# Split attention with a max-gated feed-forward on one core: a new order of all queues, with other engines for some copies and other issuers for some stores

## The chip, the core and the metric

The kernel runs on one core of one Trainium2 chip. The metric is the device time of one execution in microseconds. The core has five engines that run side by side, each through its own queue in order: TensorE (PE, with its weight loads PEld), VectorE (DVE), ScalarE (ACT), GpSimd (POOL) and SyncE (SP), which only issues DMAs here. An instruction waits on semaphores for the results it needs; while it waits, everything behind it in the same queue waits too.

## The reference

Attention with two kinds of heads, and then a feed-forward whose gate is a maximum of two projections. All is float32.

```python
# q, k, v: (4 batches, 8 heads, 768 tokens, 64); heads 0, 2, 6 are "retrieval"
scores = q @ k.T / sqrt(64)
keep   = causal                                   # retrieval heads
keep   = causal & (first 4 keys | last 64 keys)   # the other five heads
x      = softmax(where(keep, scores, -1e9)) @ v   # -> (3072 tokens, 512)
h1, h2 = x @ w1, x @ w2                           # 512 -> 1024
out    = maximum(h1, h2) @ w_out                  # (3072, 512)
```

## The kernel before, in words

**The arithmetic.** Since max(h1, h2) = h2 + relu(h1 - h2), the kernel builds w12 = w1 - w2 (L1091, on DVE) and w2o = w2 @ w_out (transposes of w2 at L1108, products at L1135, both on PE) near its start. Then out = x @ w2o + relu(x @ w12) @ w_out: one up-projection in place of two. Everything on PE is bf16, accumulated in f32 in eight PSUM banks.

**The stages.** The 3072 tokens are worked in eight half-sequences of 384 tokens, in the order (batch, half) = (0,0), (1,0), (0,1), (1,1), (2,0), (2,1), (3,0), (3,1). In each half-sequence the heads go in four pairs; a table found at run time puts the three retrieval heads first. A half-sequence passes through these steps, and several of them are in flight at once:

- SP loads q, k and v (ld, L433 and L448); DVE, ACT or POOL cast them to bf16 (qb and vb, L368 on ACT and L370 on DVE or POOL).
- q and k are turned so that the head dimension lies on the partitions (qk). In batches 0 and 1 PE does it (L595) and DVE or ACT copy the result out of PSUM; in batches 2 and 3 a DMA transpose that SP issues does it (L618).
- For the windowed heads, small copies gather the keys and values of the sinks (kx on DVE, ACT or POOL; vx likewise, L368 and L370).
- PE computes scores (L846), ACT their exponentials (at, L861), DVE multiplies by the mask (L886), PE forms the weighted sums with a column of ones for the denominator (L911), DVE takes the reciprocal (rez, L928) and normalises into x (L938).
- x is turned into xt: by PE (L1055) and a copy for the first three half-sequences, by a DMA transpose from SP (L1074) for the other five.
- PE makes the up-projection: eight groups of four matmuls (L1158), each followed by a relu into g, on ACT (L1183) or DVE (L1185).
- For each of the three tiles of 128 tokens, PE sums four x-parts (x @ w2o) and eight g-parts (g @ w_out) into one bank (L1215); ACT or DVE copies it into one of four output buffers (ot, L368 or L370, the "take-out"), and SP, ACT or POOL issues the store (out_dram<-ot, L1243).

The four output buffers tie the end of a store to a later copy: take-out number n must wait until store number n - 4 has landed. Takes 13 to 19 are stored in two DMAs of half the width.

**The front.** Until the first loads have landed and been cast, PE works on dummy matmuls (L355). In the very first half-sequence the rows of v are spread over the partitions by matmuls with a shifted identity (L638).

**What sets the order.** The function `tile_three_full_heads` (L304) builds a list of 1089 operations with their dependencies. The order in which they are emitted is a string, `PLAN` (L158), with a second string, `LAST` (L213), for the operations behind a run-time branch near the end. `Order.run` (L140) walks the string. Each token is an operation's number, a letter for its engine (p PE, a ACT, v DVE, g POOL, s SP) and, where it claims PSUM, the banks; tokens with x or y are dummies. Each engine's queue is what this walk leaves it, so the string decides the order of all five queues, which of the allowed engines makes a copy, a cast or a relu, which issuer has a store, and which bank a result goes to.

```python
n = next(i for i, c in enumerate(token) if c.isalpha())
o, e, spots = self.ops[int(token[:n])], engines[token[n]], [int(c) for c in token[n + 1:]]
for key, m in o.claims:
    self.at[key] = spots[:m]
o.emit(e)
```

Numbers of operations that are spoken of later: 618 and 613 store the tiles 10 and 9 (batch 1, second half); 828 is the DMA transpose of q and k for the third pair of (3,0), 837 that of its fourth pair, and 705 that of the fourth pair of (2,1).

Of the kernel before, what the change touches and what calls it, by code (L numbers as in the profile page):

```python
# [163 lines left out]
101v 131p7 105v 10g 108p1 132v 109p 135p3 113p 15s 145p 136a 12g 114v 110v 111v 154p 116v 143p 112v 115v 146p
117p7 119p3 118a 144p 120v 148p 121v 150p 147a 155p 151a 125v 18s 211p2 209p1 213p3 133v 210a 215p7 214a 129v
17s 149a 224p0 216a 226p4 167a 195v 169g 222p1 197a 212a 156v 157g 220p3 223a 181v 19s 173p5 201p7 221v 219p2
202a 159v 23s 174v 198a 182g 158a 218p6 183g 225v 170a 184g 168a 196g 20s 227a 189p1 163p3 160a 187p7 190v 175p5
164a 203p0 191v 229p 176a 204v 21s 188a 179v 205v 165p4 177v 207v 252p13 193v 264p50 166v 253a 200g 426s 234p
265a 162g 161v 266a 199v 254a 172g 256p74 186a 240p15 206v 258a 260p03 171g 230p 262a 185v 178g 241a 267v 237p
24s 261a 208v 192v 242a 263v 247p43 244p10 257a 217p5 194v 243v 249a 259v 246a 268p7 228p 245a 22s 255v 248a  # L170
251v 180a 269p 250v 235a 279p3 270v 284p 278p0 272v 318g 309a 273p1 285v 286v 274p 319g 280p 299a 231p 271v 275v
293g 292a 276v 277v 238a 308g 322p4 424s 281v 282v 296p6 298g 232a 287v 312p7 283v 297a 323v 302p1 428s 290p2
288p3 303a 291v 359p50 289v 363p64 377s 366p21 365a 328p3 557s 360a 338p4 301v 295g 361a 304v 311g 332p5 294v
339a 300g 367a 340p0 306v 362v 556s 364a 330p4 326v 333a 334p2 368a 435v 429g 427s 313v 397p6 436g 335a 336p5
329a 305g 341v 439p1 320g 337a 321g 342p2 233s 331v 440a 452g 451v 425s 378p73 236g 381p05 314v 343v 372p41 379a
553s 398p 316v 382a 443v 399p 307g 354p2 374a 444v 325v 560s 373a 324v 447p7 327v 383a 355p 448v 380a 310a 555s
369p01 317a 441v 389p45 384v 315g 385p37 371a 356p 390a 431g 391a 445g 558s 349p1 430a 392v 386a 455p4 376v 239a
554s 433p5 453v 350p 370a 456v 387a 552s 400p 357a 375v 503p30 401v 388v 393p47 351p 394a 403v 508s 395a 404p2
674s 434a 405p 396v 410p4 406p 411p7 457v 504a 407v 416p 402v 559s 412p 344p5 413v 505a 409v 408v 414v 490p63
676s 417v 497p02 415v 491a 418v 345p 419v 352a 506v 585g 498a 420p4 507v 677s 422p6 562a 346p 421v 353g 492a  # L180
423v 499a 432g 512p71 347v 500p04 437g 494p36 502a 561g 465p2 493v 348s 454a 501a 568g 469p5 678s 496a 449v 575g
576v 467p4 675s 470a 567v 495a 565s 459p0 578g 466v 438a 577g 528p6 514a 468v 446g 529p 513a 458g 509p53 460v
673s 516p21 524p47 515v 518a 579s 584v 461p0 563v 587a 442v 511a 473p1 462v 517a 801s 530p 566v 463p3 569a 519v
588s 526a 531p 510a 471p0 532v 474v 525a 485p2 570s 464v 472a 533v 450a 520p75 624p14 682v 803s 522a 628p30 486p
521a 806s 629a 480p5 523v 625a 527v 683a 535p7 626a 541p3 686s 534v 542p1 536p 547p 537p 543p 548v 481p 550v
581g 538v 544v 549v 540v 482p 586g 545v 687g 539v 591v 487p 546v 694g 483a 580v 551s 582v 630a 592g 627v 475p6
572g 571v 636p41 648p73 802s 640p50 564v 638a 476p 573v 642a 488v 679s 641a 681s 639v 477p 590v 649a 688v 637a
589v 650a 652p1 478a 653p 651v 680s 739p02 643v 631p57 740a 644p43 603p6 632a 691s 741a 599p0 633a 597p5 583a
805s 645a 595p2 598v 807s 646a 605p7 574v 600v 804s 596a 647v 609p4 358a 634v 704g 662p5 635v 593p3 690g 757s
701g 607p0 594v 695g 657p2 606v 608a 484g 664p 601p3 698s 665v 703a 654v 656v 697a 663p7 604a 702g 602v 658p  # L190
668p 619p0 479a 659v 660v 705s 661v 610p 667v 655v 669v 833g 670v 620p 666v 816g 671v 692v 684g 672s 611p 742v
824g 743p63 612a 811g 699v 749p21 746p57 809s 750a 621p 696g 751a 808s 834g 748a 614p4 923s 622v 745a 744a 706v
615p 685v 815v 747a 925s 810v 761p21 758p73 765p06 760a 616p 814s 766a 714p5 836g 926s 716p3 715a 927s 767a
722p0 717v 837s 762a 777p5 617v 759a 720p6 723v 778p 819s 835v 721a 779p 700v 769p32 763a 839g 768v 773p47 770a
# [1486 lines left out]
```

## Time and profile before

| what | value |
|---|---|
| median of 3 runs | 176.64 us (176.63 to 176.72) |
| the profiled execution, whole | 176.57 us |
| its span, first to last instruction | 174.8 us |
| PE busy | 166.8 us |
| DVE, ACT, POOL busy | 123.8, 112.0, 49.0 us |
| moved by DMA | 37.31 MB, 213 GB/s on average |

A row of a group reads: line, engine, operation, output<-inputs, shapes and count, then the busy time, the mean of one in ns, and the idle time of the engine just before it, with what ended most of that. A row of a timeline reads: start and length in us, engine, line, operation, output<-inputs, count, and in brackets the idle time before it and what ended that. "SPq" is the time in which SP issues a DMA, not the transfer. The chain of waits is followed back from the last instruction; each row is a start, a length, and an engine with its line or a DMA. PE's rows name the line of the matmuls; DVE's, ACT's and POOL's copies all have the line of one helper (L370 and L368), so the names of the tiles tell them apart.

### The profile page before, as it was taken

The numbers are of one execution on the slowest core, as the hardware profiler recorded it, in microseconds if no ns is written. First come the engines' busy times: TensorE is split into PE (matmuls) and PEld (weight loads), VectorE is DVE, ScalarE is ACT, GpSimd is POOL, SyncE is SP. The second block draws the span as 40 slices with busy tenths as digits, with TensorE's granted clock in tenths as the row PEclk, the third lists the DMA queues.
The fourth block names the chain that finished last, engine by engine and source line by source line (L and its number), as shares of the span: only waits on it lengthen the run. The fifth ranks groups of instructions, "written<-read, shape, count | busy, mean of one in ns | idle before, by whom it ended". The sixth has DMA issues, their size and how long they took to land.

```text
span 174.8 us, 4672 instructions
## 1 busy us (share of the span) xinstructions
PE 166.8 (95%) x1686; PEld 96.0 (55%) x1686; DVE 123.8 (71%) x342; ACT 112.0 (64%) x248; POOL 49.0 (28%) x113
## 2 busy tenths in 40 slices
PE   7999999999799999999999999999799999999992
PEld 2456555654566575566466446663456456645541
DVE  5578969698997589985958954974678728934320
ACT  3399746889969998898394286905594699200501
POOL 5722130332563103700603260100670083000300
PEclk9999999999999999999999999999999999999999
DMA  4999999999999898699999999999989563040145
GB/s 130 334 371 387 388 381 334 213 291 327 231 246 286 186 270 196 188 163 207 197 217 255 268 158 223 156 246 199 237 220 190 90 164 126 0 90 4 59 130 180
DMA packets 83677, 37.31 MB, mean 213 GB/s; under 512 B 68290, under 2 KB 78530, under 8 KB 83650
## 3 DMA queue, kind: packets, MB, share of 16 engines
q1 hardware_dynamic: 81440, 32.19, 81.9%
q0 software_dynamic: 1056, 3.15, 5.5%
q10 hardware_dynamic: 1154, 1.64, 2.8%
q8 instruction: 14, 0.23, 0.6%
q14 instruction: 13, 0.11, 0.2%
HBM read 25.17 MB, written 6.29 MB: 180 GB/s over the span
## 4 chain that ended last, share of the span: by engine, by line
PE 64%; DMA 11%; DVE 10%; SPq 7%; ACT 3%; issue 3%; DVEq 0%; ACTq 0%
PE ps L1158 21%; PE ps L1215 21%; PE ps L846 6%; PE ps L911 6%; DVE x L938 4%; SPq L618 3%; DMA qk<-qb 3%; PE ps L1135 3%; DMA ld<-in_k_dram 3%; SPq L448 3%; DMA out_dram<-ot 2%; ACT at L861 2%; PE ps L595 2%; DMA ld<-in_v_dram 2%; DVE at L886 2%
## 5 line engine op out<-in xcount | busy, mean ns | idle before, releaser
L861 ACT ACTIVATE at<-ps 128x512 bf16<-128x512 f32 (+2 forms) x134 | 65.6, 568 | 18.0 <-PE ps L846 16.4
L1215 PE MATMUL ps<-wob,g 128*128 128x512 bf16 (+2 forms) x200 | 46.3, 371 | 0.0
L1158 PE MATMUL ps<-xt,w 128*128 128x384 bf16 x256 | 45.8, 326 | 0.3 <-DVE xt L370 0.2
L1158 PEld LDWEIGHTS <-w 128*128 128x128 bf16 x256 | 23.6, 98 | 16.8 <-issue 0.8
L886 DVE TENSOR_TENSOR at<-at,tab 128x1024 bf16<-128x1024 bf16 (+5 forms) x56 | 29.1, 544 | 5.1 <-ACT at L861 4.6
L1185 DVE TENSOR_SCALAR g<-ps 128x384 bf16<-128x384 f32 x35 | 18.5, 551 | 17.7 <-PE ps L1158 15.4
L1215 PEld LDWEIGHTS <-g 128*128 128x128 bf16 x200 | 17.7, 98 | 18.6 <-issue 0.6
L1183 ACT ACTIVATE g<-ps 128x384 bf16<-128x384 f32 x29 | 14.2, 497 | 19.8 <-PE ps L1158 19.8
L370 POOL CAST qb<-ld 128x384 bf16 (+1 forms) x32 | 14.6, 477 | 42.8 <-DMA ld<-in_q_dram 29.6
L1215 PE MATMUL ps<-w2o,xt 128*128 128x512 bf16 (+2 forms) x100 | 24.3, 371 | 0.0
L938 DVE TENSOR_TENSOR x<-ps,rez 128x192 f32 x64 | 22.8, 356 | 1.7
L911 PEld LDWEIGHTS <-at 128*128 128x128 bf16 x477 | 18.5, 97 | 5.7 <-DVE at L886 1.0
L846 PE MATMUL ps<-qk 64*128 64x128 bf16 (+1 forms) x322 | 18.7, 227 | 1.6 <-DVE ot L370 1.3
L911 PE MATMUL ps<-vb,at 128*128 128x65 bf16 x387 | 19.5, 193 | 0.4 <-DVE at L886 0.3
L846 PEld LDWEIGHTS <-qk 64*128 64x128 bf16 x322 | 11.6, 94 | 10.3 <-issue 7.9
L1243 POOL DMA_DIRECT2D out_dram<-ot x18 | 9.8, 550 | 20.2 <-ACT ot L368 20.2
L370 POOL CAST vb<-ld 128x192 bf16 x26 | 9.5, 390 | 20.2 <-DMA ld<-in_v_dram 20.1
L368 ACT COPY ot<-ps 128x512 f32<-128x512 f32 (+2 forms) x13 | 7.2, 555 | 12.1 <-PE ps L1215 11.7
L1215 PEld LDWEIGHTS <-xt 128*128 128x128 bf16 x100 | 9.1, 98 | 8.9
L370 POOL COPY vx<-vb 64x396 bf16<-64x396 bf16 (+4 forms) x14 | 7.1, 511 | 21.0 <-ACT vb L368 10.4
L370 DVE COPY ot<-ps 128x512 f32<-128x512 f32 x12 | 8.1, 686 | 6.8 <-DMA out_dram<-ot 4.4
L370 DVE COPY kx<-qk 128x192 bf16<-128x192 bf16 (+5 forms) x33 | 8.5, 265 | 5.5 <-DMA qk<-qb 5.1
(76 smaller groups left out, 160.4 us busy)
## 6 DMA issues: line engine op xcount, KB each, us to landing
ld<-in_v_dram SPq DMA_DIRECT2D x21, 256.0 KB, 5.0
ld<-in_moe_w_dram SPq DMA_DIRECT2D x4, 1024.0 KB, 11.2
ld<-in_k_dram SPq DMA_DIRECT2D x4, 768.0 KB, 8.6
ld<-in_q_dram SPq DMA_DIRECT2D x4, 768.0 KB, 7.1
ld<-in_k_dram SPq DMA_DIRECT2D x12, 256.0 KB, 4.4
ld<-in_q_dram SPq DMA_DIRECT2D x12, 256.0 KB, 5.0
ld<-in_moe_w_out_dram SPq DMA_DIRECT2D x4, 512.0 KB, 6.2
out_dram<-ot POOLq DMA_DIRECT2D x6, 256.0 KB, 3.5
```

What stands on the lines that cost most here:

```text
L368: nc.scalar.copy(out=out, in_=in_)
L370: eng[e].tensor_copy(out=out, in_=in_)
L846: nc.tensor.matmul(to.rearrange("p (i c) -> p i c", c=128), lhsT=lhsT, rhs=rhs, start=True, stop=True, skip_group_check=True,)
L861: nc.scalar.activation(out=at[:, bk, 0:w], in_=bank(("ps", b, hf, t), part=bk)[:, 0:w], func=ACT.Exp, scale=scale,)
L886: eng[e].tensor_tensor(out=at, in0=at, in1=tbl, op=ALU.mult)
L911: nc.tensor.matmul(po[:, hh, i - NT * hf, :], lhsT=ats[:, T["at", b, hf, t] % NAT, bk, e * 128:(e + 1) * 128], rhs=rhs, start=first, stop= ...
L938: nc.vector.tensor_tensor(out=xs[:, HALVES.index((b, hf)) % NX, :, bass.ds(heads[2 * p + hh], 1), :], in0=po[:, hh, :, 0:D].unsqueeze(2), ...
L1158: nc.tensor.matmul(bank(key)[:, 0:HALF], lhsT=w[:, kc, fc * 128:(fc + 1) * 128], rhs=xts[:, HALVES.index((b, hf)) % NXT, :, kc, :], start= ...
L1183: nc.scalar.activation(out=g, in_=ph, func=ACT.Relu)
L1185: nc.vector.tensor_scalar_max(out=g, in0=ph, scalar1=0.0)
L1215: nc.tensor.matmul(bank(key)[:, cols], lhsT=lhsT, rhs=(w2o if kind == "x" else wob)[:, c, cols], start=(e == 0), stop=(e == len(steps) - 1),)
L1243: queues[e].dma_start(out=out[r0:r0 + 128, lo:lo + n], in_=ots[:, number % NOUT, lo:lo + n])
```

## The change

Only the strings `PLAN` and `LAST` are replaced. The list of operations and their dependencies are the same, and so is every function.

```diff
 PLAN = """
-1s y0 0s y0 2s y0 y1*3 y2*3 3s y3*3 y4 29a 51v y4 57a 59v y4 49a 67v y5 27v 65g 54p0 62p1 y7 55v 25g y7 y2*2 y7
...
+0s y0 1s y0 2s y0 y1*2 3s y1 y2*3 y3*3 28a 64v y4*2 48v y4 26v y5 58v y5 50g y5 y6*3 y7*2 49a 29v 51g y7 27a
...
 LAST = """
-1074v 1068p 1075a 1077p 1069v 1078p 1070s 1081p5 1079a 1082p 1083p 1080s 1084a 1085a
+1069a 1074v 1077p 1070s 1078p 1075s 1081p7 1079a 1082p 1083p 1080s 1084a 1085a
```

By engine, DVE has 311 operations in place of 316, ACT 272 in place of 253, POOL 76 in place of 91, SP 94 in place of 93. PE has the same operations with 30 dummies in place of 27. Of the relus ACT has 36 in place of 29, of the take-outs 16 in place of 13, and DVE the rest. Of the stores SP has 7 in place of 6, ACT 9 in place of 7, POOL 9 in place of 12, not always the same ones. The first load is of q, not of k.

SP's queue in the part in which the first loads and transposes of the last two batches' second halves are issued, before the change. The transposes of qk are L618, that of x is L1074, the stores are L1243:

```order
L618 DMA_TRANSPOSE qk<-qb 128x6x128
L448 DMA ld<-in_k_dram 128x8x64 x2
L618 DMA_TRANSPOSE qk<-qb 128x6x128 x2
L1243 DMA out_dram<-ot 128x512
L448 DMA ld<-in_v_dram 128x8x64
L448 DMA ld<-in_q_dram 128x8x64
L618 DMA_TRANSPOSE qk<-qb 128x6x128
L1243 DMA out_dram<-ot 128x512
L448 DMA ld<-in_q_dram 128x8x64
L1074 DMA_TRANSPOSE xt<-x 128x12x128
```

The same part of SP's queue after the change:

```order
L1074 DMA_TRANSPOSE xt<-x 128x12x128
L448 DMA ld<-in_q_dram 128x8x64
L618 DMA_TRANSPOSE qk<-qb 128x6x128 x3
L448 DMA ld<-in_k_dram 128x8x64
L448 DMA ld<-in_q_dram 128x8x64 x2
L448 DMA ld<-in_k_dram 128x8x64
L618 DMA_TRANSPOSE qk<-qb 128x6x128
L448 DMA ld<-in_k_dram 128x8x64
L618 DMA_TRANSPOSE qk<-qb 128x6x128
L448 DMA ld<-in_v_dram 128x8x64
L1074 DMA_TRANSPOSE xt<-x 128x12x128
```

The two stores (613 and 618) are no longer in SP's queue. The transpose 705, which stood ahead of the first rows shown of before, is the second of the three in the third row shown of after, behind the xt, the q load and the transpose 837.

POOL's queue after the change, around the stores that it takes over; qb and vb are casts, vx is a copy of sink values:

```order
L370 COPY vx<-vb 64x198
L1243 DMA out_dram<-ot 128x512
L370 ISA
L370 COPY qb<-ld 128x6x64
L370 ISA
L370 COPY vb<-ld 128x3x64
L370 COPY vx<-vb 64x2x198
L370 ISA
L370 COPY vb<-ld 128x3x64
L1243 DMA out_dram<-ot 128x512
```

The first of the two is 618, the second 613. Each stands in POOL's queue among casts that wait for loads.

ACT's queue in the last stage, before the change, up to the run-time branch; g is a relu, ot a take-out:

```order
L1183 ACTIVATE g<-ps_163 128x384
L1183 ACTIVATE g<-ps_160 128x384
L368 COPY ot<-ps_158 128x512
L1183 ACTIVATE g<-ps_161 128x384
L1183 ACTIVATE g<-ps_163 128x384
L1243 DMA out_dram<-ot 128x256 x2
```

The same part after the change:

```order
L368 COPY ot<-ps_157 128x512
L1183 ACTIVATE g<-ps_158 128x384
L1243 DMA out_dram<-ot 128x256 x2
L368 COPY ot<-ps_156 128x512
L1183 ACTIVATE g<-ps_162 128x384
L1183 ACTIVATE g<-ps_160 128x384
L368 COPY ot<-ps_161 128x512
L1183 ACTIVATE g<-ps_157 128x384
L1243 DMA out_dram<-ot 128x256 x2
L1183 ACTIVATE g<-ps_159 128x384
L1183 ACTIVATE g<-ps_162 128x384
L1183 ACTIVATE g<-ps_156 128x384
```

Four of the last eight relus were ACT's; now seven are, with two take-outs and two stores in two parts standing between them, and DVE has one.

More of the change, by code (lines that the diff above doesn't have):

```diff
@@ L164 @@
[L164 to L193, printed above, removed]
@@ new lines @@
+79v 137p0 84v 94a 88v 97p5 140p 90a 96v 99p 91a 139p4 100v 107p2 102v 98p1 130a 92v 141p 142p 134v 131p3 101v
+109p 10v 103p 132a 135p5 153p 104v 15s 106v 136a 110v 108p3 111v 113p 145p 112v 12a 143p 114v 116v 144p 115v
+154p 105v 17s 150p 117p5 121v 119p2 146p 120a 148p 118v 155p 125v 211p3 156a 18s 209p1 129v 213p2 215p5 212v
+133v 222p6 216a 19s 210a 220p3 223a 224p5 167a 159v 214a 147v 226p1 157a 197v 169a 218p6 181v 195a 183v 221a
+225v 149a 20s 201p2 163p0 151v 187p3 219p5 182a 198g 170a 168g 188v 196a 21s 184g 227a 202v 173p7 158g 203p4
@@ new lines @@
+160a 175p3 189p1 204v 174a 229p 22s 190a 205v 164v 176a 264p27 207v 191v 165p4 265a 193v 260p13 23s 177v 266a
+172g 252p02 166v 199a 234p 171g 254a 162g 186a 267v 200a 185g 261a 256p74 255v 230p 161g 258a 194v 179v 428s
+257a 180v 208v 247p21 192v 262a 237p 259v 248a 263v 253a 278p4 249a 280p 244p73 250v 24s 240p20 281v 178a 206v
+217p1 241a 292v 282v 242a 251v 279p2 283v 284p 228p 245a 285v 243v 235a 424s 287v 246a 273p0 236g 293v 298a
+268p4 286v 269p 274p 238a 296p7 309g 270v 426s 275v 231p 272v 318a 319g 276v 297a 308g 271v 322p6 553s 299g 277v
@@ new lines @@
+429v 387a 437v 375v 394a 558s 378p73 376v 389p45 457v 380a 431v 350p 401v 388v 379a 395a 351p 402v 403v 390a
+557s 396v 404p6 391a 433p3 384v 410p7 352a 392v 405p 560s 412p 434a 344p1 413v 414v 441v 508s 411p2 415v 416p
+406p 417v 490p45 559s 407v 503p03 409v 491a 345p 353s 408v 504a 418v 492a 675s 419v 500p74 494p60 420p2 566g
+496a 422p5 561g 421v 346p 423a 442g 562v 239a 576g 465p0 347v 505a 565s 567g 463p2 495a 585v 466a 432v 459p5
+464v 502a 673s 506v 501a 512p31 509p60 568g 493v 676s 513a 497p24 461p7 510a 348s 454v 575v 511a 469p3 458g 449v
@@ new lines @@
+777p6 612v 837s 614p7 759a 693g 760a 703v 615p 751a 813v 750a 778p 705s 826a 779p 780p 761p45 781v 765p21 835v
+752p03 814s 616p 753a 763a 710p0 617a 927s 720p5 754a 711v 924s 618g 767a 712p7 764v 923s 825g 840v 766a 782v
+716p3 704g 783v 816a 926s 706v 768v 714p0 707a 721v 708p1 717a 819s 755v 836a 838v 718p2 697v 709a 713v 700g
+762a 769p65 715v 893p31 818g 770a 773p74 613g 722p0 771a 925s 774a 729p6 772v 828s 775a 756v 790p5 723a 791p7
+776v 784p4 894a 785p 786p 895a 792p 796p 787v 734p0 793v 719a 794v 930s 797v 789v 730p 799v 795v 731p 798v 788v
@@ new lines @@
+989a 906p2 941v 869p 866a 904v 946v 945a 905v 907p 870p 908v 915v 910v 1001p75 909v 992p03 991v 1002a 995p14
+921s 858p2 952v 996a 955v 1004v 956g 997a 859p 949v 871a 1006s 993a 860p 1003a 994a 1022p71 861v 998p46 1014p05
+1000a 1026p3 1005v 862g 1027p 999a 1028p 1023a 959p2 1015a 967p6 960v 1016a 1029p 1024a 971p4 968v 939a 1007p70
+972v 942g 1010p25 1018p61 1009a 1030v 957p4 1031v 1012a 1017v 1019a 961p0 1025v 1011a 963p5 958a 1013v 1020a
+1039p6 969p2 1008a 1021v 1033p4 970a 978p1 964a 962a 1040p7 1045p 1041p 1034p 1046v 1032v 1035p 965p2 1042v
```

47 lines of the change are left out of this document (26 added, 21 removed).

## The prediction

> **What bounds the kernel now.** I read the first page first: the span, the busy time of each engine and the chain that ended last.
>
> ```profile
> span 174.8 us, 4672 instructions
> PE 166.8 (95%) x1686; PEld 96.0 (55%) x1686; DVE 123.8 (71%) x342; ACT 112.0 (64%) x248; POOL 49.0 (28%) x113
> PE 64%; DMA 11%; DVE 10%; SPq 7%; ACT 3%; issue 3%; DVEq 0%; ACTq 0%
> ```
>
> PE is busy for 95% of the span, and no other engine passes 71%. The operations do not change, so PE's busy time cannot change by much either: an order can only win or lose in the 174.8 - 166.8 = 8.0 us in which PE does nothing, which include the start before the first matmul and the last store's way to memory. The list of waits says who holds PE, and what holds those in turn.
>
> ```profile
> PE ps L846 <- DVE ot L370: 1.3, 1, 1.3
> PE ps L1055 <- DVE x L938: 1.1, 3, 0.8
> ...
> DVE kx L370 <- DMA qk<-qb: 5.1, 3, 2.1
> ...
> DVE ot L370 <- DMA out_dram<-ot: 4.4, 2, 4.1
> ```
>
> PE's longest single wait is for a copy of an output tile (L370, ot) out of PSUM by DVE. The second is for normalised rows (L938, x) that it is to turn. DVE itself waits for two kinds of transfers: turned q and k (qk<-qb), and stores that free an output buffer (out_dram<-ot). The busy times by window show in which stages PE has room: columns are the window, its length, then the busy time of PE, PEld, DVE, ACT, POOL, the granted clock, the DMA share and GB/s.
>
> ```profile
> 27.10:49.70 22.60, 21.17 (x232) 13.02 (x232) 20.08 (x49) 17.83 (x44) 7.08 (x19) 1.00 1.06 278
> 105.70:125.60 19.90, 18.46 (x212) 10.76 (x213) 14.33 (x40) 10.43 (x26) 2.81 (x6) 1.00 1.24 211
> 158.60:171.60 13.00, 13.00 (x81) 7.26 (x79) 4.90 (x11) 2.71 (x6) 1.61 (x3) 1.00 0.23 77
> ```
>
> The first two leave PE idle for 1.43 and 1.44 us. The last stage has no hole at all: there a reorder can only lose. The clock is 1.00 throughout, so nothing is to be had from it.
>
> **Term a: the two stores that leave SP's queue (105 to 125 us).** These rows are SP's queue, DVE and PE around PE's longest wait, and the store's landing in the chain.
>
> ```profile
> 110.33 4.35 SPq L618 DMA_TRANSPOSE qk<-qb  x2
> ...
> 116.60 1.71 SPq L618 DMA_TRANSPOSE qk<-qb  x1
> 118.41 0.52 SPq L1243 DMA_DIRECT2D out_dram<-ot  x1
> ```
> ```profile
> 107.73 0.68 DVE L370 COPY ot<-ps 128x512 f32<-128x512 f32 x1
> ...
> 122.00 0.26 DVE L370 COPY kx<-qk 128x320 bf16<-128x320 bf16 x1 [2.11 <-DMA qk<-qb]
> ...
> 122.75 0.69 DVE L370 COPY ot<-ps 128x512 f32<-128x512 f32 x1 [0.24 <-DMA out_dram<-ot]
> ```
> ```profile
> 123.50 0.38 PE L846 MATMUL ps<-qk 64*128 64x128 bf16 x7 [1.25 <-DVE ot L370]
> ```
> ```profile
> 118.41 4.26 DMA out_dram<-ot
> ```
>
> The output tile was ready at 107.73 + 0.68 = 108.41, but its store stood in SP's queue behind transposes that take 1.7 to 2.2 us each to issue, and went at 118.41: 10.0 us in the queue, 4.26 us on the way. It landed at 122.67; the copy that needed its buffer began at 122.75, and PE's scores, which needed the bank emptied by that copy, had waited 1.25 us. In the new order this store (618) and the one before it (613) are POOL's, right behind the copies that fill them, and POOL is busy 28% of the span. The store then lands about 10 us earlier relative to its copy, long before the buffer is asked for again. But the same DVE queue also waited 2.11 us, until 122.00, for a transpose that SP issued at 116.60; without the store, the output copy could have begun at about 122.5, only 0.3 us sooner, had the transpose stayed where it is. The new order has SP issue this transpose (828) without stores ahead of it and with more PE work between it and its reader (5.6 us against 3.9, an estimate counted along PE's queue with the durations of this trace), which is as much as 1.7 us to set against that wait of 2.11. I take the stall as gone: -1.3. Bounds: 0, if the transpose's landing holds DVE as now; -1.4, all that the window leaves.
>
> Against this speaks the Trainium skill, "DMA: Bandwidth & Descriptors", section "Issuing engines are not separate DMA queues": transfers from any issuer share the same 16 engines, and spreading issuers saves only the issue time, usually small beside the transfer. By that rule term a is near 0, which is the first rival below. Here the trace disagrees on "small": 10.0 us in the queue against 4.26 on the way.
>
> **Term b: the turn after the second half-sequence (44 to 50 us).** The chain of waits there:
>
> ```profile
> 44.40 0.57 PE ps L911 x13
> ...
> 46.53 0.20 DVE rez L928
> ...
> 47.53 0.36 DVE x L938
> 47.89 0.52 DVE qk L370
> ...
> 49.74 4.06 PE ps L1158 x24
> ```
>
> After the last weighted sum at 44.97 DVE still has the normalisations of three tiles ahead of PE's turn, and copies of turned x behind it, until the next up-projection at 49.74. The new order leaves two tiles' normalisations (two instructions of 0.36 us fewer) behind the last weighted sum, turns the first two tiles first and gives ACT one of the copies of turned x. So -0.7. Bounds: -1.1 (all that PE waits for x at L1055) and 0, if another copy takes the place.
>
> **Term c: the front.** PE before 13 us:
>
> ```profile
> 1.15 5.52 PE L355 MATMUL ps<-warmer 128*128 128x512 bf16 x16 [1.15 <-POOL warmer L1606]
> 6.73 0.51 PE L595 MATMUL ps<-tab,qb 128*128 128x128 bf16 x6
> 7.08 1.89 PE L355 MATMUL ps<-warmer 128*128 128x512 bf16 x8
> ...
> 11.50 0.40 PE L846 MATMUL ps<-qk 64*128 64x128 bf16 x8
> 12.22 1.02 PE L638 MATMUL ps<-xt,g 128*128 128x512 bf16 x4 [0.33 <-DVE xt L370]
> ```
>
> Now 26 dummies stand ahead of the first turn, where 16 stood; by the rows the ten more end at about 1.15 + 5.52 + 10 x 0.23 = 9.0 us, where the first turn was at 6.73. The dummies fill time in which PE would wait for loads, so the three that are added (30 against 27) cost nothing by themselves. But the spreading of v (L638) waits for casts of v, at 12.22 as now, and ahead of it stands one group of scores where three stood: up to two groups of 0.40 us go behind it and are done later, of which I take about half: +0.4. Bounds +0.8 (both groups) and -0.3 (the 0.33 that PE waits there, if the casts come sooner).
>
> **Term d: the last stage.** ACT and DVE, PE's x-part of the down-projection, the two groups of ACT and the last store's issue:
>
> ```profile
> 162.65 0.87 ACT L1183 ACTIVATE g<-ps 128x384 bf16<-128x384 f32 x2 [12.80 <-PE ps L1158]
> ...
> 172.05 0.34 ACTq L1243 DMA_DIRECT2D out_dram<-ot  x1
> ```
> ```profile
> 163.95 1.49 DVE L1185 TENSOR_SCALAR g<-ps 128x384 bf16<-128x384 f32 x3 [2.36 <-PE ps L1158]
> ```
> ```profile
> 160.50 4.06 PE L1158 MATMUL ps<-xt,w 128*128 128x384 bf16 x24
> 164.40 1.89 PE L1215 MATMUL ps<-w2o,xt 128*128 128x512 bf16 x8
> ```
> ```profile
> L1183 ACT ACTIVATE g<-ps 128x384 bf16<-128x384 f32 x29 | 14.2, 497 | 19.8 <-PE ps L1158 19.8
> L368 ACT COPY ot<-ps 128x512 f32<-128x512 f32 x11 | 6.5, 588 | 5.9 <-PE ps L1215 5.7
> ```
>
> Today the last eight relus are four on each engine. In the new order ACT has seven, with two output copies and two stores in two parts between them: 7 x 0.50 + 2 x 0.59 + 4 x 0.34 = 6.0 us from the second up-projection's end. PE needs the last relu after six more ups and two x-parts, 4.06 + 1.89 = 5.95 us. ACT so ends level or a little late; with some 0.2 us from a matmul's end to a relu's start and as much back, +0.5. Bounds 0 (the g-parts take the late tile last) and +1.3 (the stores' waits for issue also fall between).
>
> **Term e: SP between 98 and 108 us.** SP, and DVE behind it:
>
> ```profile
> 98.08 3.69 SPq L618 DMA_TRANSPOSE qk<-qb  x2
> 101.86 1.47 SPq L1074 DMA_TRANSPOSE xt<-x  x1
> 103.38 1.53 SPq L448 DMA_DIRECT2D ld<-in_v_dram  x2
> ```
> ```profile
> 103.08 0.40 DVE L370 COPY kx<-qk 128x192 bf16<-128x192 bf16 x1 [2.04 <-DMA qk<-qb]
> ...
> 107.25 0.56 DVE L1185 TENSOR_SCALAR g<-ps 128x384 bf16<-128x384 f32 x1 [2.24 <-PE ps L1158]
> ```
>
> The second transpose at 98.08 (705, the last of the sixth half-sequence) is now put behind five transfers that followed it: the xt, two v loads, a q load and another transpose (837), at 1.47 + 1.53 + 0.8 + 1.9 = 5.7 us of issue. Its reader on DVE, the copy of kx, also stands later, but 4.4 us of PE work behind the issue where it was 5.0: 0.6 less cover. Behind that copy DVE holds relus of the running stage that PE waits for; today a wait of 2.04 costs PE nothing, for DVE then waits 2.24 us on PE. I take +0.4 of the missing 0.6; bounds 0 and +1.4.
>
> The rest goes together at 0: ACT takes 19 more operations and DVE 5 fewer, both below 75% busy; the remaining stores change issuers with PE work of over 3 us to cover them.
>
> **Sum.** -1.3 - 0.7 + 0.4 + 0.5 + 0.4 = -0.7. The profiled execution took 176.57 us, its span 174.8 and 1.77 around it; the median of the runs shown is 176.64, 0.07 above it. So the span becomes 174.1 and the time 175.9 us.
>
> **Rivals.**
> - The transpose's landing holds DVE at 120 us, not the store: term a is 0, the sum +0.6, the time 177.2. For it: the 2.11 us wait came first and the store's own 0.24 was on top. Against it: two stores leave the queue ahead of that transpose. Chance 0.17. By the rule of the Trainium skill in term a the time is this one too.
> - Slower, by one mechanism: the transpose 705 lands too late. If SP's slip is half as much again as the 5.7 us of issue (2.9 more), DVE holds the relus behind the copy for 2.9 - 0.6 = 2.3 us that PE sees; term e is +2.3 in place of +0.4, and the time is 175.9 + 1.9 = 177.8. It decides from a landing past about 110 us. For it: DVE's waits on these transposes are its largest on a transfer (5.1 us). Against it: two stores fewer in that queue. Chance 0.16.
> - All of the idle time in the two windows goes and nothing new comes: -1.4 - 1.1 = -2.5, 174.1 us. Against it: the last stage and the front offer new waits. Chance 0.12.
> - The new order does nothing that shows, since PE is 95% busy in both and the idle time only changes place: 176.6. Chance 0.10.
>
> **The numbers.** My forecast, 175.9, has the chance 0.45, with its own range of 175.0 to 177.0. A measurement of this kernel can tell 0.2%, 0.35 us, from no change: faster is below 176.29, slower above 176.99. Of the forecast's 0.45 some 0.35 is faster, 0.07 the same, 0.03 slower. With the third rival faster has 0.47; with the fourth and a part of the first (0.03) the same has 0.20; slower has 0.33. The range, 174.0 to 178.2, takes in the first two rivals with the 0.4 us that the other terms may add, and the third.
>
> **What would show it.** Term a: PE's wait on DVE's ot copy is gone from the list of waits, and the stores that POOL issues there land within 6 us of their copies. Term b: under 0.5 us of PE waiting for x at L1055. Term c: PE's wait at L638 grows. Term d: PE, which has no hole after 158 us, waits for ACT's relus near its end. Term e: DVE waits for qk<-qb with a wait of PE on a relu behind it. I am wrong if the sum of PE's idle time within the span moves by other places than these, or if PE's busy time itself changes by over 0.5 us.

## The result, and the profile after

The new order is slower. Over 20 executions of each, the ratio to the kernel before is 1.0057, with a 95% interval of 1.0031 to 1.0084: about 1.0 us on 176.64, where 0.7 us less was forecast. The profiled execution took 177.17 us, 0.60 us more than that of before. Executions of this kernel scatter (175.99 to 181.45 us), so the ratios leave disturbed ones out, and no time is taken from the four profiles of disturbed ones (the transpose of x earlier, the cast with it, fewer dummies, v by POOL with it), only the places and lengths of waits and stages and the clock.

The head of the page after the change answers to the one shown of before:

```profile
span 175.4 us, 4665 instructions
PE 166.5 (95%) x1666; PEld 96.2 (55%) x1689; DVE 117.3 (67%) x337; ACT 119.6 (68%) x265; POOL 42.1 (24%) x95
PE 53%; DMA 25%; DVE 10%; issue 4%; SPq 4%; POOL 1%; ACT 1%; DVEq 0%; POOLq 0%; ACTq 0%
```

PE is as busy as before. What changed is the chain that ended last: DMA has 25% of it where it had 11%. The list of waits shows the same thing from PE's side:

```profile
DVE kx L370 <- DMA qk<-qb: 6.1, 4, 2.4
...
PE ps L1158 <- DMA xt<-x: 1.0, 1, 1.0
...
PE ps L846 <- DVE x L938: 0.9, 2, 0.6
```

The wait for an output copy (1.3 us) and the waits for x at PE's turn (1.1 us) are gone, as forecast. In their place PE waits for a DMA transpose of x (xt<-x) and for normalised rows at the scores. The busy times by stage say where the time went. First the kernel before, then the new order (the second number behind the window is PE):

```profile
27.00:50.00 23.00, 21.53 (x234) 13.21 (x234) 20.45 (x51) 18.23 (x45) 7.38 (x20) 1.00 1.06 277
...
80.00:97.00 17.00, 17.00 (x197) 10.33 (x196) 13.01 (x39) 11.07 (x27) 5.32 (x12) 1.00 1.14 221
97.00:126.00 29.00, 27.48 (x276) 14.75 (x273) 20.00 (x58) 15.53 (x37) 6.30 (x15) 1.00 1.20 210
126.00:140.00 14.00, 13.91 (x126) 7.74 (x123) 10.71 (x30) 9.91 (x24) 3.97 (x9) 1.00 0.93 173
```
```profile
27.00:50.00 23.00, 22.40 (x238) 13.75 (x240) 21.07 (x56) 19.24 (x49) 6.62 (x17) 1.00 1.01 265
...
80.00:97.00 17.00, 15.30 (x154) 8.63 (x155) 11.12 (x33) 13.09 (x31) 3.00 (x5) 1.00 1.21 210
97.00:126.00 29.00, 28.27 (x288) 15.94 (x290) 19.38 (x56) 18.29 (x44) 9.28 (x20) 1.00 1.08 216
126.00:140.00 14.00, 13.06 (x127) 7.42 (x127) 8.24 (x28) 10.30 (x24) 2.02 (x4) 1.00 0.56 150
```

The new order wins 0.87 us of PE work at 27 to 50 us, loses 1.70 at 80 to 97, wins 0.79 at 97 to 126 and loses 0.85 at 126 to 140. Beside these stand three dummies more at the front. These are differences of busy time: they show where PE stood still, and over all windows they sum to the change of PE's busy time (166.8 to 166.5), not to the 0.6 us of the span. The two losses are two places. At the first, DVE, SP and PE of the new order read:

```profile
84.92 0.36 DVE L370 COPY kx<-qk 128x128 bf16<-128x128 bf16 x2 [1.27 <-DMA qk<-qb]
85.20 0.34 DVE L938 TENSOR_TENSOR x<-ps,rez 128x192 f32 x1
```
```profile
85.57 1.44 SPq L1074 DMA_TRANSPOSE xt<-x  x1
```
```profile
85.59 0.29 PE L846 MATMUL ps<-qk 64*128 64x128 bf16 x4 [0.59 <-DVE x L938]
...
90.73 2.77 PE L1158 MATMUL ps<-xt,w 128*128 128x384 bf16 x16 [1.01 <-DMA xt<-x]
```

DVE waits for a transpose of q and k; behind the waiting copies stands the last normalisation of (1,1), and behind that the transpose of x, which PE needs at about 89.7 us and gets at 90.7. In the old order that transpose was issued at 85.37, landed at 89.53, and PE began the up-projection that reads it at 89.86: it was just in time.

```profile
85.37 1.44 SPq L1074 DMA_TRANSPOSE xt<-x  x1
```

At the second place:

```profile
131.26 0.36 DVE L370 CAST qb<-ld 128x384 bf16 x1
...
137.02 0.22 DVE L370 COPY kx<-qk 64x192 bf16<-64x192 bf16 x1 [1.96 <-DMA qk<-qb]
137.27 0.36 DVE L938 TENSOR_TENSOR x<-ps,rez 128x192 f32 x1
```
```profile
138.21 0.77 PE L846 MATMUL ps<-qk 64*128 64x384 bf16 x4 [0.35 <-DVE x L938]
139.39 1.02 PE L1215 MATMUL ps<-w2o,xt 128*128 128x512 bf16 x3 [0.41 <-DVE x L938]
```

A cast of q (operation 936, on ACT in the old order) now stands on DVE behind a normalisation for which DVE waits on PE. The transpose 940 needs it, is issued as it ends, at 131.65, and lands at 137.0 where it landed at 134.3; the copy of kx waits for that, with five normalisations of (3,0) queued behind it.

### The profile page after: what moved, and what is told of

Same layout as the page of the kernel before. It is cut to its first block, busy times and chain, and to the rows that moved or that the text cites. A ratio compares the mean times of both kernels' runs of the same rounds, so it can differ in the third digit from the quotient of the medians.

```text
span 175.4 us, 4665 instructions
## 1 busy us (share of the span) xinstructions
PE 166.5 (95%) x1666; PEld 96.2 (55%) x1689; DVE 117.3 (67%) x337; ACT 119.6 (68%) x265; POOL 42.1 (24%) x95
## 4 chain that ended last, share of the span: by engine, by line
PE 53%; DMA 25%; DVE 10%; issue 4%; SPq 4%; POOL 1%; ACT 1%; DVEq 0%; POOLq 0%; ACTq 0%
PE ps L1215 21%; PE ps L1158 16%; DMA qk<-qb 9%; DMA ld<-in_moe_w_dram 7%; DMA ld<-in_k_dram 5%; PE ps L911 5%; PE ps L355 5%; PE ps L846 4%; DMA xt<-x 3%; DVE x L938 2%; PE ps L595 2%; SPq L448 2%; DVE g L1185 2%; SPq L618 1%; DVE w L1091 1%
## 5 line engine op out<-in xcount | busy, mean ns | idle before, releaser
L1158 PE MATMUL ps<-xt,w 128*128 128x384 bf16 x256 | 44.9, 326 | 1.1 <-DMA xt<-x 1.0
L886 DVE TENSOR_TENSOR at<-at,tab 128x1024 bf16<-128x1024 bf16 (+5 forms) x56 | 27.1, 512 | 4.5 <-ACT at L861 4.3
L370 POOL CAST qb<-ld 128x384 bf16 (+1 forms) x28 | 13.2, 495 | 43.4 <-DMA ld<-in_k_dram 38.2
L1183 ACT ACTIVATE g<-ps 128x384 bf16<-128x384 f32 x36 | 16.8, 498 | 7.1 <-PE ps L1158 6.5
L846 PE MATMUL ps<-qk 64*128 64x128 bf16 (+1 forms) x322 | 19.5, 227 | 1.3 <-DVE x L938 0.9
L368 ACT COPY ot<-ps 128x512 f32<-128x512 f32 (+2 forms) x16 | 9.1, 569 | 16.4 <-PE ps L1215 16.0
L1185 DVE TENSOR_SCALAR g<-ps 128x384 bf16<-128x384 f32 x28 | 15.1, 550 | 6.4 <-PE ps L1158 6.0
L846 PEld LDWEIGHTS <-qk 64*128 64x128 bf16 x322 | 11.7, 94 | 12.2 <-issue 9.2
L1243 POOL DMA_DIRECT2D out_dram<-ot x12 | 6.6, 552 | 34.9 <-ACT ot L368 22.5
L368 ACT CAST qb<-ld 128x192 bf16 (+1 forms) x25 | 10.1, 442 | 6.3 <-issue 2.5
L370 DVE COPY ot<-ps 128x512 f32<-128x512 f32 x9 | 6.2, 691 | 8.9 <-PE ps L1215 8.1
L370 POOL CAST vb<-ld 128x192 bf16 x21 | 7.7, 385 | 17.8 <-DMA ld<-in_k_dram 11.3
```

What stands on the lines that cost most here:

```text
L368: nc.scalar.copy(out=out, in_=in_)
L370: eng[e].tensor_copy(out=out, in_=in_)
L846: nc.tensor.matmul(to.rearrange("p (i c) -> p i c", c=128), lhsT=lhsT, rhs=rhs, start=True, stop=True, skip_group_check=True,)
L886: eng[e].tensor_tensor(out=at, in0=at, in1=tbl, op=ALU.mult)
L1158: nc.tensor.matmul(bank(key)[:, 0:HALF], lhsT=w[:, kc, fc * 128:(fc + 1) * 128], rhs=xts[:, HALVES.index((b, hf)) % NXT, :, kc, :], start= ...
L1183: nc.scalar.activation(out=g, in_=ph, func=ACT.Relu)
```

## The experiments

Sixteen kernels, each against runs of the kernel before on the same chip. The first four repair or redo one part alone. Their source is two lines shorter, so L844 there is L846 here, and so on.

**The normalisation ahead of the waiting copies, at the first place** (new order):

```diff
-548v 549v 591v 486p 589v 550v 483a 627v 551s
+548v 549v 550v 591v 486p 589v 483a 627v 551s
```

> The new order, with one instruction moved: the last normalisation of (1,1) stands ahead of the copies of kx that wait for a DMA transpose of q and k, not behind them. Theory (the copies' wait of 1.27 us, until the transpose landed at 84.90, held that normalisation, and with it the DMA transpose of x, which was issued at 85.57 and landed at 90.69): PE's waits of 0.59 at 85.6 us and 1.01 at 90.7 us both go, about 1.9 us with their edges, and the ratio to the kernel before falls from 1.0057 to about 0.995. Rival (SP's queue is what delays the transpose of x): it is issued less than 0.5 us sooner and PE still waits for it by 0.7 us or more; the ratio stays at 1.003 or above.

The ratio was 1.012 (1.0083 to 1.0156): not faster. SP's and PE's rows there:

```profile
85.73 2.97 SPq L1072 DMA_TRANSPOSE xt<-x  x1
```
```profile
91.92 2.77 PE L1156 MATMUL ps<-xt,w 128*128 128x384 bf16 x16 [2.21 <-DMA xt<-x]
```

DVE had finished x at 83.9, but SP was still busy with the transfers ahead, issued the transpose of x at 85.73 as before, and it took 6.2 us to land in place of 5.1. The rival held: at this place the queue of transfers was as late as DVE. That the ratio is higher than the new order's goes with the clock: five of its eleven executions show a mean granted clock of 0.98 to 0.99 (three of the new order's twenty do), and the other six have a median of 178.24 us, 0.8% above the old order's 176.83, as the new order's other seventeen have (177.78 against 176.45).

**The copy of kx behind the normalisations, at the second place** (new order):

```diff
-906p2 941v 869p 866a 904v 946v 945a 905v 907p 870p 908v 915v 910v 1001p75 909v
+906p2 869p 866a 904v 946v 945a 905v 907p 870p 908v 915v 910v 909v 941v 1001p75
```

> The new order, with the second place mended alone: the copy of kx that waits until 137.0 us for a DMA transpose stands behind the last normalisations of (3,0), not ahead of six of them. Theory: PE's waits of 0.35 and 0.41 for x at 138 to 139.4 us go, 1.5 us with their edges, and the ratio is about 0.997. Rival (the scores that need the copy wait instead, as the copy now comes last): PE waits for kx at 138 us by 0.5 us or more, and the ratio stays within 0.002 of 1.0057.

The ratio was 1.0128 (1.0074 to 1.0183). PE's waits for x are gone, and the scores that need the copy wait instead, as the rival said:

```profile
141.31 0.23 PE L844 MATMUL ps<-qk,kx 64*128 64x128 bf16 x1 [0.59 <-DVE kx L368]
```

The place at 91 us was worse in this run too: PE waited 1.08 us for x and 2.53 us for xt. Nothing was changed ahead of it, so this is scatter: four profiles with the same program up to there, the new order's, this one and two below (the cast ahead, the stores back), have 1.6, 3.6, 2.7 and 2.2 us of waits at 85 to 92 us. What a repair of this place does can't be read from one profile's length of the wait.

**Both together.**

> The new order with both places mended. Theory (two separate stalls of one kind): the gains add up, 1.9 + 1.5 = 3.4 us, the ratio is about 0.986 and the kernel is faster than both, near 174.0 us. Rival (the time that is won early is lost again at the next place that waits for transfers): less than 2 us come through, the ratio is 0.995 or above.

The ratio was 1.006 (1.0023 to 1.0097); the rival held. The wait for xt had grown to 3.24 us, and the matmuls behind it took 4.14 us where 2.77 is usual:

```profile
92.21 4.14 PE L1156 MATMUL ps<-xt,w 128*128 128x384 bf16 x16 [3.24 <-DMA xt<-x]
```

With this the theory that DVE's order at the two places is the cause fell. Two questions were left: whether transfers set the pace there, and what made 940 late.

**The two stores to POOL, in the old order.**

```diff
-612a ... 613s ... 617v ... 618s
+612a 613g ... 617v 618g
```

> The kernel before with one part of the change alone: the stores 613 and 618 are issued by POOL right behind the copies that fill them, not by SP behind transposes. Theory of the prediction (the store's landing holds the output copy): PE's wait of 1.25 us at 123.5 goes, the ratio is about 0.993. Rival (the landing of the transpose that DVE waits for holds the copy): DVE still waits until about 121 us, as SP gains only the two stores' issue of 0.52 us each; PE keeps 0.3 us or more of its wait there, and the ratio is 0.995 to 0.998.

The ratio was 1.0018 (0.9986 to 1.0051): no gain, not even the 0.2% and more that the rival allowed. DVE still waits for the transpose and PE for DVE:

```profile
122.64 0.26 DVE L368 COPY kx<-qk 128x320 bf16<-128x320 bf16 x1 [1.98 <-DMA qk<-qb]
```
```profile
123.81 0.38 PE L844 MATMUL ps<-qk 64*128 64x128 bf16 x7 [0.91 <-DVE ot L368]
```

The store itself no longer appears as a wait, and nothing is won: term a was put on the wrong one of two transfers that ended 0.7 us apart.

**The transpose of x one transfer earlier** (new order, with the first repair):

```diff
-630a 801s 545v 547p 482p 694a 580v 548v 549v 591v 486p 589v 550v 483a 627v 551s
+630a 545v 547p 482p 694a 580v 548v 549v 550v 591v 486p 589v 483a 627v 551s 801s
```

> The new order with the last normalisation of (1,1) ahead of the copies of kx, and with the transpose of x behind it put one transfer earlier in SP's queue (ahead of a load of q that is needed much later). Theory (where SP's queue stands sets when x arrives): the transpose is issued at about 84 to 85 us and lands by 90, PE's wait for it is under 1.0 us where it was 2.21 with the normalisation alone moved, and the ratio falls from 1.012 to 1.006 or below. Rival (the transfers as a whole are the limit, whatever their order): it lands at 91 us or later again, and the ratio stays above 1.009.

The ratio was 1.0027 (0.9977 to 1.0077), which does not tell it from the new order. In the profile the transpose was issued at 83.99 and landed at 88.75, as the theory said, and PE did not wait for it. But PE then waited 1.47 us at 103 for a cast of v, 0.41 at 108 for the next transpose of x, and 0.66 and 1.09 us at 113 to 115.

**The cast ahead of the normalisation** (new order):

```diff
-917p 727a 902p 913p 856p0 918v 936v
+917p 727a 902p 913p 856p0 936v 918v
```

> The new order with one cast moved on DVE: the cast of q (936) that feeds the late transpose 940 stands ahead of a normalisation for which DVE waits on PE, not behind it. Theory (940 was issued at 131.65, right behind its cast at 131.26 to 131.62, so the cast's place made it late): it is issued near 130 and lands near 134.5 in place of 137.0, PE's waits of 0.35 and 0.41 for x at 138 to 139.4 us go, and the ratio falls by about 0.008 from 1.0057. Rival (transfers set the pace there): it lands at 136.5 us or later, and nothing changes.

The ratio was 1.0002 (0.9958 to 1.0045), 0.0055 below the new order; the two intervals overlap. The issues of SP at 131.4 us, with the median from issue to landing, in this run and then in the new order at 131.65:

```profile
qk<-qb SPq DMA_TRANSPOSE x1, 3.1
```
```profile
qk<-qb SPq DMA_TRANSPOSE x1, 5.3
```

It landed at 134.53, and PE waits for nothing between 115 us and its end. The stages ahead ran about 1.2 us later in this profile, so the 0.23 us by which it was issued sooner are 1.4 us by the work; the other part is the landing, which was 2.2 us shorter. That the landing is on the forecast of 134.5 is luck, since the issue was expected near 130. What the cast is worth is best read from the stage: the time from the up-projection of one half-sequence to that of the next, in the new order and then in this run.

```profile
125.52 3.41 PE L1158 MATMUL ps<-xt,w 128*128 128x384 bf16 x20
...
143.52 1.47 PE L1158 MATMUL ps<-xt,w 128*128 128x384 bf16 x8
```
```profile
126.72 3.41 PE L1158 MATMUL ps<-xt,w 128*128 128x384 bf16 x20
```

In this run the next one began at 143.22, so the stage is 18.00 us in the new order and 16.50 here. All profiles of the new order and its variants say the same: 16.50 or 16.51 us in the five with the cast ahead, 17.95 to 18.16 in the six that leave this stage as it is in the new order (that one among them), and 17.35 in the two with the copy of kx moved. So the late cast costs 1.5 us.

**Half the loads of batches 2 and 3**, in the new order and in the old:

```diff
-                    out=lds[:, s, at, :, i * D:i * D + D],
-                    in_=src[b, :, r0:r0 + 128, :].rearrange("h p d -> p h d"),
+                    out=lds[:, s, at, 0:(4 if b > 1 else H), i * D:i * D + D],
+                    in_=src[b, 0:(4 if b > 1 else H), r0:r0 + 128, :].rearrange("h p d -> p h d"),
```

> The new order with the loads of q, k and v of batches 2 and 3 cut to the first four heads (the other heads keep what lay in the buffer, so the result is not the reference's); every other instruction is as it was. Theory (the transfers are a second limit between 60 and 140 us, and the new order loses there what it wins at 47 us): PE's waits at 85, 91, 107, 113, 138 and 139 us, 4.4 us in all, nearly go, and the time is near 173.5 us, lower than that of the old order with the same loads by 1 us or more. Rival (the order of DVE and ACT is itself what makes PE wait): 2 us or more of those waits stay, and the new order stays level with or above the old one.

> The kernel before with the same loads cut to four heads. Theory (the stall at 122 us is the transposes' landing): PE's wait of 1.25 us there goes and little else changes, near 174.8 us. Rival (it is the place of the store and of the copies in the queues): the wait stays at 0.8 us or more, and the time is above 175.8 us.

The new order's ratio was 0.9879 (0.982 to 0.9937), median 174.36 us; the old order's 0.9935 (0.9902 to 0.9967), median 175.42. With room for its transfers (a DMA share of 0.83 and 0.87 at 80 to 126 us, where it was 1.12 and 1.18) the new order is the better one by about a microsecond; its six executions took 172.90 to 175.18 us, the old order's twelve 174.56 to 176.92. PE's list of waits in it is nearly empty (first the new order with half the loads, then the old):

```profile
PE ps L1215 <- DVE x L938: 0.5, 1, 0.5
...
PE ps L846 <- DVE x L938: 0.4, 1, 0.4
```
```profile
PE ps L1055 <- DVE x L938: 1.1, 3, 0.8
...
PE ps L911 <- DVE x L938: 0.9, 1, 0.9
```

The waits at 85, 91, 107 and 113 us are gone, and what is left in the new order are the two at the late cast, as that doesn't hang on loads (with these two, the new order's waits are 2.8 us in all and not the 4.4 of the expectation). In the old order the wait of 1.25 us at 122 has gone too: it was transfers, though here the store and the transpose both land sooner, so that this run does not say which. Its waits at the turn (L1055) stay, as they should.

**The cast and the transpose of x together** (new order).

> The new order with both repairs that moved a transfer: the cast of q (936) ahead of the normalisation, and the transpose of x of (1,1) one transfer earlier with its last normalisation ahead of the copies of kx. Theory (each repair removes its own stall): the waits at 91 us and at 138 to 139 us are both gone and the ratio is 0.992 to 0.996. Rival (SP's transfers between 60 and 125 us are a second limit, and what is put ahead of a load makes that load late): the wait at 91 goes, new waits for casts and relus appear between 100 and 117 us, and the ratio is within 0.003 of the 1.0002 that the cast alone gave.

Neither wait is what it was (0.25 us is left at 89 us, nothing near 138), and new ones have come, as the rival said: 1.03 us at 103 us for a cast of v, 0.87 at 108 for the next transpose of x, 0.74 and 0.38 at 114 to 115 for relus.

```profile
89.24 2.77 PE L1158 MATMUL ps<-xt,w 128*128 128x384 bf16 x16 [0.25 <-DMA xt<-x]
```

The ratio of 0.9904 (0.9841 to 0.9967) would be the theory's, but the median of all 12 executions was 177.62 us, against 176.98 of the old order: the time is undecided.

**The stores back to SP** (new order):

```diff
-617a 927s 720p5 754a 711v 924s 618g ... 613g ... 819s ... 828s
+617a 927s 720p5 754a 711v 924s ... 819s 613s ... 828s 618s
```

> The new order with the stores 613 and 618 given back to SP, behind the transposes 819 and 828. Theory of the prediction (these stores' place is worth 1.3 us): PE waits for an output copy near 122 to 124 us by 1 us or more, and the ratio is about 1.013. Rival (the landing of the transpose 828, until 121.6 us, is what held PE in the old order, and the store lands within half a us of it): PE's new wait there is below 0.5 us and the ratio is within 0.003 of 1.0057.

The ratio was 1.0007 (0.9965 to 1.0048), a little below even the rival's range, and PE does not wait at 122 to 124 us at all, though DVE does:

```profile
122.03 0.36 DVE L370 COPY kx<-qk 128x128 bf16<-128x128 bf16 x2 [2.52 <-DMA qk<-qb]
```

So the wait that the new order is rid of there did not go with the stores. Other work of PE that now stands at that time is what is left as the reason; no run moved it alone. The ratio is also as low as that of the cast ahead, though the cast is late here (its stage took 18.12 us): a difference of 0.005 between two of these ratios is not the mark of one cause.

**Four dummies fewer ahead of the first turn** (new order; `y6*3` and one `y5` left out).

> The new order with four of the 26 dummies ahead of the first turn left out (30 to 26 in all). Theory (the first turn waits for casts that end at 8.9 to 9.4 us, so the dummies fill time that PE would wait): the first turn begins at 8.8 us or later, the spreading of v at about 12.1 us as before, and the ratio stays within 0.002 of 1.0057. Rival (PE is bound at the front by the dummies): everything comes 4 x 0.22 = 0.9 us sooner and the ratio is about 1.001.

The ratio was 1.0042 (0.9996 to 1.0089). The first turn waits, as the theory said, for a cast, and the spreading of v began at 11.90 where it was 12.09:

```profile
8.97 1.36 PE L595 MATMUL ps<-tab,qb 128*128 128x128 bf16 x21 [0.65 <-DVE qb L370]
```

**Two loads more behind the transpose of x** (as the cast and the transpose, with 803s and 806s behind 551s).

> As the run with cast and xt, and two further loads for (3,0), of k and q, also put behind the transpose of x. Theory (SP's order sets what arrives when, and these loads are needed late): the transposes 588 and 686 land one to two transfers sooner, DVE's wait near 85 us is under 0.5 us, PE waits nowhere by over 0.5 us between 80 and 100 us, and the ratio is 0.990 to 0.995. Rival (the transfers' sum is the limit): the loads put back are late in turn, casts of (3,0) wait, PE waits between 100 and 130 us, and the ratio is 0.998 or above.

PE waits nowhere between 80 and 100 us, as the theory said; and then this:

```profile
103.64 0.41 PE L911 MATMUL ps<-vb,at 128*128 128x65 bf16 x8 [2.38 <-ACT vb L368]
```

The ratio was 1.0067 (1.003 to 1.0103), the rival's. What the queue gives at one place it took back at the next: 2.38 us for a cast of v whose load came late.

**The late cast alone, in the old order:**

```diff
-890a 947s 876v 939g 936a ... 940s ... 954s ... 918v
+890a 947s 876v 939g ... 954s ... 918v 936v 940s
```

> The kernel before with one part of the change alone: the cast of q (936) goes from ACT to DVE, behind the normalisation 918, and the transpose 940 that needs it so comes behind 954 in SP's queue. Theory (the place of this cast costs the time at 138 us): 940 is issued at about 136 us in place of 130.67 and lands near 140, PE waits for the copy of kx by 2 to 4 us near 140 us, and the ratio is 1.010 to 1.02. Rival (the old order has cover for it): PE waits less than 1 us and the ratio is below 1.004.

The ratio was 1.0193 (1.0153 to 1.0232). PE's waits, and the windows around them, in which the number behind POOL's is the granted clock:

```profile
138.44 0.23 PE L846 MATMUL ps<-qk 64*128 64x128 bf16 x1 [1.69 <-DMA qk<-qb]
139.09 0.29 PE L846 MATMUL ps<-qk 64*128 64x128 bf16 x2 [0.41 <-DVE x L938]
```
```profile
138.00:140.00 2.00, 1.14 (x9) 0.54 (x10) 1.55 (x5) 0.29 (x1) 0.00 (x0) 0.70 0.00 0
140.00:142.00 2.00, 2.00 (x6) 0.76 (x5) 0.74 (x3) 0.77 (x2) 0.00 (x0) 0.50 1.02 153
142.00:144.00 2.00, 2.00 (x19) 0.90 (x19) 0.00 (x0) 1.40 (x5) 0.60 (x2) 0.95 0.46 97
```

The cast's place, with the transpose behind another one in SP's queue, makes the old order slower, by more than the new order lost. The waits were at the low end of what was expected (2.1 us in all) and the ratio at the high end, for the clock: the windows lack (0.30 + 0.50 + 0.05) x 2.00 = 1.70 us of full clock. Waits and clock are 3.8 us together. From the up-projection at 125.20 us to the one at 145.15 this run took 19.95 us; the old order took 16.29 for the same stage (125.56 to 141.85), 3.66 less.

**Six loads of v by POOL** (the new order with the cast ahead; the same with the transpose of x; the old order):

```diff
-V_QUEUES = ()
+V_QUEUES = ((2, 1, "POOL"), (3, 0, "POOL"), )
...
-679s 680s 681s 807s 808s 809s
+679g 680g 681g 807g 808g 809g
```

> The new order with the cast (936) ahead, and the six loads of v of (2,1) and (3,0) issued by POOL in place of SP. Theory A (SP's own queue, in which one transfer lands every 1.1 us, is the second limit): the transposes of qk and x behind these loads come sooner, PE's waits near 86, 91 and 114 us fall below 0.5 us each, and the ratio is 0.985 to 0.992. Theory B (the 16 DMA engines together are the limit): the transposes land as before within 1 us, the waits stay, and the ratio is within 0.004 of 1.0002.

> The same with the transpose of x of (1,1) one transfer earlier as well (and its last normalisation ahead of the copies of kx). Theory A: with the v loads out of SP's queue, the waits that this repair brought at 103 to 115 us do not come, PE waits nowhere by over 0.5 us between 80 and 130 us, and the ratio is 0.98 to 0.99, faster than both kernels. Theory B: PE waits again for casts or relus between 100 and 117 us by 2 us or more in all, and the ratio is 0.997 or above.

> The kernel before with the same six loads of v issued by POOL. Theory A: the transpose that lands at 121.97 lands 2 us or more sooner, PE's wait of 1.25 us at 123.5 goes, and the ratio is 0.990 to 0.994. Theory B: it lands within 1 us of that, the wait stays above 0.7 us, and the ratio is 0.997 or above.

The ratios were 1.0131 (1.0083 to 1.0179) for the first and 1.0107 (1.0057 to 1.0157) for the old order; the second ran at a median of 183.95 us. Theory A fell, and the first is slower than Theory B said, too. Between 80 and 100 us, issue to landing took, first with the six loads on POOL and then in the new order with all on SP (with the cast ahead and all on SP, which differs from the first by the issuer alone, it is 4.6 and 4.9):

```profile
ld<-in_v_dram POOLq DMA_DIRECT2D x6, 256.0 KB, 8.4
...
qk<-qb SPq DMA_TRANSPOSE x4, 6.2
```
```profile
ld<-in_v_dram SPq DMA_DIRECT2D x6, 256.0 KB, 4.5
...
qk<-qb SPq DMA_TRANSPOSE x4, 4.5
```

A second issuer did not add room here: these loads and the transposes took longer to land, and a transpose that must be soon now shares the engines with loads that could wait. In the old order PE's wait of 1.25 us at 123.5 did go, as Theory A had it, but the transpose landed at 122.56 where it was 121.97, as B had it, and PE came 1.7 us later, for a wait where there was none; with the transpose of x earlier there was one of 8 us:

```profile
92.14 3.42 PE L1158 MATMUL ps<-xt,w 128*128 128x384 bf16 x20 [2.40 <-DMA xt<-x]
```
```profile
108.58 0.48 PE L846 MATMUL ps<-cp 64*128 64x384 bf16 x1 [7.96 <-DVE x L938]
```

SP's one queue is thus not only a limit but also the order of arrival that the kernel needs.

## Why the prediction was wrong, point by point

The sign was wrong: 0.7 us faster was forecast, and it is 0.6 us slower between the two profiles and about 1.0 by the ratio. The step that failed is "The rest goes together at 0": the sum has no term for the two places that decide. One is the cast 936, moved behind a normalisation, which costs 1.5 us. The other is what PE meets when it comes sooner from the turn: at 85 to 92 us it waits for transfers, 1.6 us in the profile, and these waits are gone with half the loads. The range of 174.0 to 178.2 held the time, and the first rival's 177.2 was near it, by luck: that rival keeps PE's wait at 122 us, which went, and has neither of the two losses. The least difference that the prediction took as measurable, 0.2%, was also too small: the interval over 20 executions is 0.27% to each side.

- **Term a failed in its cause.** The prediction said: "I take the stall as gone: -1.3." PE's wait did go, but not by the stores: the same move gave nothing in the old order (1.0018), and undoing it cost nothing in the new (1.0007). What held DVE, and PE behind it, in the old order was the transpose's landing, as the first rival had it: with the stores on POOL DVE still waited for it, until 122.64. The 1.7 us of more PE work that were to be set against DVE's wait for the transpose do not show on DVE either: it waited 2.43 us, until 121.60, where it had waited 2.11, until 122.00. That PE lost nothing by it is the part that no run explains alone. The rule of the Trainium skill, "DMA: Bandwidth & Descriptors", section "Issuing engines are not separate DMA queues", that issuers share the 16 engines, speaks the same way as these runs, and as the slower runs with v on POOL. The trace's 10.0 us in SP's queue was right and proved nothing, since nobody needed the store before 122 us; nor did it speak against that rule, which is about the time of an issue (0.52 us for this store), while the 10.0 us are the wait behind other issues.
- **Term b was right, and larger than taken, and was lost again.** PE's waits at L1055 are gone (1.1 us), PE did 0.87 us more by 50 us, and the up-projection behind the turn began at 48.89 where it began at 49.74. But the up-projection that waits at the first place began at 90.73 where it began at 89.86: what PE gains by 50 us it gives up at 85 to 91, where it meets the transfers. This is the step that the prediction did not make: having said that DVE waits for transfers, it did not ask what a PE that comes earlier would wait for next.
- **Term c was near in size, not in its sign.** PE is 0.38 us busier by 27 us, but three dummies of 0.22 us more are 0.65, so it is about 0.3 us behind in real work where +0.4 was taken; the up-projection at 27.10 began at 27.38. But PE's wait at L638, which was to grow, is gone, and the spreading began at 12.09 where it began at 12.22. Four dummies fewer changed its start by only 0.2.
- **Term d was too high: it is 0.** ACT's last four relus took 1.80 us together, 0.45 each and not 0.50, and the stores' issue ran beside ACT's work and not in it. The 0.2 us from a matmul's end to a relu's start were too much as well: in the kernel before, PE's up-projection ended at 160.50 + 4.06 = 164.56 and ACT's relu behind it began at 164.60, 0.04 us later. In the new order:

```profile
163.07 0.59 ACT L368 COPY ot<-ps 128x512 f32<-128x512 f32 x1
163.35 0.45 ACTq L1243 DMA_DIRECT2D out_dram<-ot  x1
163.54 1.80 ACT L1183 ACTIVATE g<-ps 128x384 bf16<-128x384 f32 x4
```

  The last relu ended at 165.34, ahead of PE's first g-part at 165.99, and PE does not wait for it; adding the four issues to ACT's time was the mistake.
- **Term e was right in size.** PE waited 0.29 us at 113.2 us for a relu of DVE, where +0.4 was taken. The transpose 705 landed at 110.43, past the limit of about 110 that the second rival names, and the 2.3 us of that rival did not come: DVE's wait there was 0.45 us, for the transpose ahead of it.
- **"The rest goes together at 0" failed.** In it was the cast 936, moved from ACT to DVE behind a normalisation that waits on PE. It feeds the transpose 940, which feeds a copy that holds five normalisations. Putting that one cast back in front shortened the stage by 1.5 us and gave a ratio of 1.0002; putting it behind in the old order cost 1.9%, about half of it by the clock. The cost of this one token is as large as the whole loss, though the places that wait for transfers lose as much in the profile.

The account as the runs leave it: the new order wins about 1 us at the turn, cannot keep it because transfers arrive no sooner, and loses 1.5 us at one cast. Open stays what makes landings differ between executions of the same program (with the first repair most were 0.4 to 0.9 us later from 65 us on, well ahead of the place that was changed), and no version with the reference's result was found that is clearly faster than both.

## What to carry to other kernels

When a second resource is nearly as full as the first (here transfers, with a DMA share of 1.0 to 1.2 in most windows from 27 to 126 us beside a PE at 95%), a reorder that brings the first one forward can just move its wait to the next place where the two meet, as here from 47 to 91 us: look for the landings that PE now reaches with a fraction of a microsecond to spare, and cost the gain against those. Of a moved operation, follow the whole chain behind it, cast to transpose to copy to whatever stands in that queue, and not only its own engine. Of two transfers that end close together in front of a wait, take neither as the cause before one of them has been moved alone.

## What the runs showed of the hardware

A long wait of PE can cost more than its length. Behind waits of 2.49, 2.53 and 3.24 us (and of 1.69 and 0.41 close together) the granted clock fell to about 0.5; in the profiles with waits of 2.38 and 2.40 us it did not. In each of the four, windows of 2 us as shown for the late cast lack 1.70 us of full clock, which is 3.4 us at half. With four dummies fewer, 16 matmuls behind the wait of 2.49 us took 4.34 us where they took 2.77 in the new order.

No threshold can be read from this. Of the twelve executions of the kernel whose profile has the wait of 2.38 us and a clock of 1.00, nine show a mean clock of 0.988 to 0.990, about what one such fall leaves (1.70 of 176 us are 0.0097); of 103 executions of the kernel before, beside the experiments, four do.

The Trainium skill, "TensorE: Matmul & The Clock Gate", section "Part 1: The HAM clock gate", says that the array's clock halves after an idle window of about 3.4 us. The half is what the windows show; the waits here were shorter than that figure, but for the one of 7.96 us.

The transpose 940 took 5.30 to 5.45 us from issue to landing in the eight kernels in which SP issued it after the transpose ahead of it had landed (5.35 in the new order, 5.30 with half the loads, 5.37 with the stores back on SP, 5.42 with the first repair), and 2.94 to 3.14 us in the five with the cast ahead, where that one was still on its way (3.11 with the cast ahead alone). An empty queue is not the whole reason: the transpose of x that SP issued at 139.40 in the new order, with nothing in flight, took 3.72 us. What makes the difference is open.
